# Four constants of a list scheduler's account: longer and later loads, transposes placed further back, weight-block sums one unit later

One core of one Trainium2 chip. The metric is device time in microseconds of one execution. Before: median 419.47 us of three runs (418.99 to 419.58).

## The reference

Sigmoid attention, then a gated feed-forward block:

```python
# q, k, v: [8, 12, 448, 64]; x: [3584, 768]; d_ff = 1536
scores = q @ k.transpose(0, 1, 3, 2) / 8 - log(448)
attn_out = sigmoid(scores) @ v                       # no softmax: no row sums
x = attn_out.transpose(0, 2, 1, 3).reshape(3584, 768)
g = x @ w_gate
out = (g * sigmoid(g)) * (x @ w_val) @ w_out
```

## The kernel before

The program cuts the attention into 24 units of four heads (q, k and v of one unit are 448 KB each), each with scores and the product of their sigmoids with v (PV), both in 64x64 tiles of the TensorE where all else has 128x128, and the feed-forward block into 96 pairs of a gate and a value product. The output product uses seven products for eight, for which some 128-row blocks of w_out are added and subtracted first: the **weight-block sums**, twelve instructions on DVE.

Every instruction is entered as an `Op` with an engine, a duration, its dependencies and the buffers that it takes and gives. A list scheduler plays these durations through, at each moment takes for each engine the first ready operation in a window of its queue, and emits all in the order in which it started them. The durations are an account, in the program text, of what the chip will do. On the chip every engine runs its own list in order and waits at semaphores, so a wrong duration gives no wrong result, only a poor order.

The account of loads and the constants that the change touches:

```python
class Op:
    def __init__(self, eng, dur, fn, deps=(), ..., desc=(0, 0)):
        ...
        n, size = desc                       # pieces and bytes of a piece
        self.hold = n == 1792
        self.dma = 2.0 if n == 1792 else n / 16 * max(0.042, 0.003 + size / 24600)

LAT = {"PE": 0.2, "ACT": 0.15, "DVE": 0.13, "POOL": 0.25, "SP": 1.7}
...
MARGIN = 0.0
...
# in list_schedule, for a load: the loads queue behind one another
                if o.dma:
                    dma = max(dma, now + 0.5) + o.dma
                    ...
                    o.t1 = dma + LAT["SP"]
...
# transposes on PE, units 0 to 5; -MARGIN makes them ready so much later
            a = op("PE", 0.06 * (s1 - s0), fpe(s0, s1),
                   deps=[(ins[min(k, len(ins) - 1)], -MARGIN if i > QB else 0.0)], ...)
...
    loads(0, "qk")
    ...
    loads(1, "qk")
    R["st_k", 0][1].dma += 1.0
    R["st_q", 1][0].dma += 0.4
```

The weight-block sums are drawn from a generator, one in each quarter of a unit; output products begin when the last is in the list:

```python
WSN = 1
            if i > WO + 4 or i == WO + 4 and sl > 1:      # WO = 4
                for _ in range(WSN):
                    next(wsums, None)
...
            f2acc = f2acc + 12.5 / 22.0 if f2q else 0.4
            while f2q and f2acc >= f2q[0][0] and ("ws", 4, NH - 2) in R:
                w, fn = f2q.pop(0)
                f2acc -= w
                fn(not att)
```

PE idle gaps that the account itself foresees at the start are filled with matmuls on zeros (`ps_warm`).

Of the kernel before, what the change touches and what calls it, by code (L numbers as in the profile page):

```python
# [19 lines left out]
class Slot:  # L20
# [3 lines left out]
    def __init__(self, tag):  # L24
        self.tag, self.t1 = tag, None


class Op:
# [3 lines left out]
    def __init__(self, eng, dur, fn, deps=(), mode=("F", "F"), take=(), give=(), desc=(0, 0)):  # L32
        self.eng, self.dur, self.fn, self.mode = eng, dur, fn, mode
        self.deps = [d if isinstance(d, tuple) else (d, 0.0) for d in deps if d is not None]
        self.take = [Slot(t) for t in take]
        self.give = list(give)
        self.rank = self.t0 = self.t1 = None
        n, size = desc
        self.hold = n == 1792
        self.dma = 2.0 if n == 1792 else n / 16 * max(0.042, 0.003 + size / 24600)  # L40

    def got(self, tag):
        return [s for s in self.take if s.tag == tag]
# [12 lines left out]
NEAR = 12  # L56
VIS = 9
WO = 4
MARGIN = 0.0
FREE = set()  # L60


# [90 lines left out]
def kernel(  # L153
# [70 lines left out]
    def op(*a, **kw):  # L224
        o = Op(*a, **kw)
        ops.append(o)
        return o
# [11 lines left out]
    R = {}  # L239
# [76 lines left out]
    def cast_wc(c):  # L316
        for nm in ("wg", "wv"):
            R["w16", nm, c] = [op("POOL", 0.85, fc, deps=[ld], give=ld.take)
                               for fc, ld in R["w", nm, c]]
# [8 lines left out]
    def cast_wo(f):  # L328
        R["wo16", f] = op("POOL", 0.85,
                          lambda: nc.gpsimd.tensor_copy(out=wo16[:, f], in_=T["wo", f]),  # L330
                          deps=[R["wo", f]], give=R["wo", f].take)
# [5 lines left out]
    def tr_pe(i, n, parts=None, tag="TO", split=False):  # L337

        ins = R[("cq", "ck")[n], i]
        parts = parts or [("DVE", 0, NS)]  # L340

        def fpe(s0, s1):
            def fn():
                if s0 == 0 or split:
                    T["tr", i, n] = psum.tile([128, NS, 128], BF16, tag=tag, bufs=2, name="ps_tr")
                T["tr", i, n, s0] = T["tr", i, n]
                for s in range(s0, s1):
                    nc.tensor.transpose(out=T["tr", i, n][:, s, :],  # L348
                                        in_=src16[i % NSRC][:, n, s].rearrange("p a d -> p (a d)"),
                                        identity=idn)  # L350
            return fn

        def fm(eng, s0, s1):
            def fn():
                if n == 0 and s0 == 0:
                    qkT_tile(i)
                cp(eng, T["qkT", i][:, n, s0:s1], T["tr", i, n, s0][:, s0:s1])
            return fn
        for k, (eng, s0, s1) in enumerate(parts):
            a = op("PE", 0.06 * (s1 - s0), fpe(s0, s1),  # L360
                   deps=[(ins[min(k, len(ins) - 1)], -MARGIN if i > QB else 0.0)],
                   take=[tag] if s0 == 0 or split else [], give=R["cq", i][0].take if n and s1 == NS else [])
            if s0 == 0 or split:
                bank = a.take
            m = op(eng, 0.1 + (0.53 if eng == "DVE" else 0.8) * (s1 - s0) / NS, fm(eng, s0, s1), deps=[a],
                   take=["qkT"] if n == 0 and s0 == 0 else [], give=bank if s1 == NS or split else [])
            R.setdefault(("qkT", i), []).append(m)
            R["qkT", i, n, s0] = m
# [12 lines left out]
    def burst(ds):  # L381


        def fpe():
            for i, s in ds:
                sc = psum.tile([128, 2, 512], FP32, tag="A", bufs=2, name="ps_sc")
                qT, kT = T["qkT", i][:, 0], T["qkT", i][:, 1]
                for g in range(2):
                    for a in range(2):
                        r = slice(64 * a, 64 * a + 64)  # L390
                        nc.tensor.matmul(  # L391
                            out=sc[64 * (g ^ a):64 * (g ^ a) + 64, a, 0:S].rearrange("k (s p) -> k s p", s=NS),
                            lhsT=kT[r, s, 64 * g:64 * g + 64], rhs=qT[r, :, 64 * g:64 * g + 64],
                            start=True, stop=True)
                T["sc", i, s] = sc
        give = [x for i, s in ds if s == NS - 1 for x in R["qkT", i][0].got("qkT")]
        deps = [x for i in {i for i, _ in ds} for x in R["qkT", i]]
        if ds[0][0] == 0:
            deps = [x for k, x in R.items() if k[:2] == ("qkT", 0) and len(k) > 2 and (k[2] == 0 or k[3] <= ds[0][1])]
        a = op("PE", 0.03 + 0.19 * len(ds), fpe, deps=deps,  # L400
               mode=("Q", "Q"), take=["A"] * len(ds), give=give)
        for n, d in enumerate(ds):
            sig(d, (a, 0.19 * (len(ds) - 1 - n)), a.take[n])
# [272 lines left out]
    def loads(i, which="qkv"):  # L676
        for nm in which:
            load(i, nm, {"q": q, "k": k, "v": v}[nm], [0, 3, NS] if i == 0 and nm == "k" else None)
# [7 lines left out]
    op("ACT", 1.5, lambda: nc.scalar.activation(out=warm, in_=sb_t, func=SIGM))  # L686
    loads(1, "qk")
    R["st_k", 0][1].dma += 1.0
    R["st_q", 1][0].dma += 0.4
    loads(0, "v")  # L690
    def fill(n):

# [19 lines left out]
    def bursts(i, sl):  # L712

        if i >= NQ:
            return []
        if i < QB:
            return [[(i, s)] for s in range(2 * sl, min(2 * sl + 2, NS))]
        if i < VIS and (i - QB) % 2 == 0:
            return [[(i, 2 * sl), (i, 2 * sl + 1)]] if sl < 3 else [[(i, 6), (i + 1, 0)]]
        if i < VIS:  # L720
            return [[(i, 2 * sl + 1), (i, 2 * sl + 2)]] if sl < 3 else []
        return {0: [[(i, 0), (i, 1)], [(i, 2)]], 1: [[(i, 3), (i, 4)]], 2: [[(i, 5), (i, 6)]], 3: []}[sl]
# [11 lines left out]
    for i in range(NQ + QB + 2):  # L734
        att = i < NQ
        for sl in range(4):
            if i < QB:
                nf = 0
            elif i < QB + 4:
                nf = 1 if sl < 3 else 0  # L740
            else:
                nf = min(2, max(0, 4 * (i - QB) + sl - LAG - fpos + 1))
            if i < NCW and sl == 3:
                cast_wc(i)
            if WO < i <= WO + 4 and sl == 1:
                for f in range(3 * (i - WO - 1), 3 * (i - WO)):
                    cast_wo(f)
            if i > WO + 4 or i == WO + 4 and sl > 1:
                for _ in range(WSN):
                    next(wsums, None)  # L750
            fs = []
            while len(fs) < nf and fpos < B * NF and ("xT", fpos // NF, KC - 1) in R:
                fs.append(divmod(fpos, NF))
                fpos += 1
            vals = []
            if fs and (sl or fs[0] == (0, 0)):
                vals.append(f1(*fs[0]))
            for n, ds in enumerate(bursts(i, sl)):
                if n == 1 and i >= VIS:
                    pv(i - 1)  # L760
                burst(ds)
            if sl == 0 and (i == NQ or QB < i < VIS):
                pv(i - 1)
            if sl == 0 and 0 < i < QB:
                pv(i - 1)
            if sl == 3 and i == QB - 1:
                pv(i)
            if att and i + 1 < NPE and sl in (1, 2):
                tr_pe(i + 1, sl - 1)
            if fs and not vals:  # L770
                vals.append(f1(*fs[0]))
            for n, (b, f) in enumerate(fs):
                if n:
                    vals.append(f1(b, f))
                vals[n]()
                if b % 2 == 1 and f == NF - 1:
                    f2q.extend(f2_items(b // 2))
            if att and sl == 0 and i + 2 < NQ:
                casts(i + 2)
            if att and sl == 1 and NPE <= i + 2 < NQ:  # L780
                tr_dma(i + 2)
            if sl == 1:
                if AHEAD <= i + 3 < NQ:
                    loads(i + 3)
                if WO <= i < WO + 4:
                    for f in range(3 * (i - WO), 3 * (i - WO + 1)):
                        load_wo(f)
                    uses[1] = uses[0]
# [5 lines that stand above are left out]
# [50 lines left out]
```

## Time and profile before

| | before |
|---|---|
| time, median of 3 | 419.47 us |
| time of the execution that was profiled | 420.82 us (span of the trace 419.0) |
| busy PE, DVE, ACT, POOL | 410.4, 237.7, 217.5, 133.3 us |
| DMA from 10 to 50 us | full, 375 to 382 GB/s |

Engines are PE (TensorE), DVE (VectorE), ACT (ScalarE), POOL (GpSimd), SP (SyncE, which issues the loads). The row of forty digits gives busy tenths of equal slices of the span. An instruction in order of time reads: start us, duration us, engine, line, operation, output<-input, shapes, count, and in brackets how long the engine had idled before it and whom it waited for. The lines are in the prediction below.

### The profile page before, as it was taken

To read this page: it belongs to the slowest core of one execution; us is meant where nothing else is said; L and a number is where in the kernel's file an instruction comes from. 1 tells how busy PE (TensorE), PEld (TensorE's weight loads), DVE (VectorE), ACT (ScalarE), POOL (GpSimd) and SP (SyncE) were. 2 spreads that over 40 slices of the span, in tenths; PEclk is the share of its full clock that TensorE was granted. 3 is DMA by queue.
4 is the path that set the end of the run, shared out by engine and by line. 5 is a ranking of instruction groups with operands and counts; after the bars stand their busy time and mean duration, and the time that the engine had idled before them with its cause. 6 is when DMAs were issued, how large, how long until landed. Compare 5 with 4: busy or idle time off the path is not lost.

```text
span 419.0 us, 7945 instructions
## 1 busy us (share of the span) xinstructions
PE 410.4 (98%) x3194; PEld 205.1 (49%) x3194; DVE 237.7 (57%) x420; ACT 217.5 (52%) x290; POOL 133.3 (32%) x196
## 2 busy tenths in 40 slices
PE   8989999999999999999999999999999999999995
PEld 3434444444445554544454554554545545555563
DVE  3544544467667644564574745647556465565873
ACT  5986778778751165467445565455455552122000
POOL 1788865764360232424031431403400100000000
PEclk9999999999999999999999999999999999999999
DMA  8999999997980284488067373482500302020235
GB/s 266 380 375 377 375 286 340 314 314 184 229 248 2 76 215 83 150 172 236 2 177 125 127 223 74 140 144 100 120 2 0 77 2 75 2 74 1 60 95 150
DMA packets 64693, 66.97 MB, mean 160 GB/s; under 512 B 35536, under 2 KB 60880, under 8 KB 64656
## 3 DMA queue, kind: packets, MB, share of 16 engines
q1 hardware_dynamic: 62704, 59.39, 49.7%
q0 software_dynamic: 1632, 6.69, 6.3%
q8 instruction: 25, 0.41, 0.4%
q10 hardware_dynamic: 320, 0.39, 0.3%
q14 instruction: 12, 0.10, 0.1%
HBM read 47.19 MB, written 11.01 MB: 139 GB/s over the span
## 4 chain that ended last, share of the span: by engine, by line
PE 90%; DMA 6%; DVE 1%; ACT 1%; SPq 0%; issue 0%; POOL 0%; POOLq 0%
PE ps_g L466 26%; PE ps_v L466 23%; PE ps_o L599 18%; PE ps_sc L391 8%; PE ps_pv L426 7%; PE ps_ol L599 5%; DMA st<-in_k_dram 4%; PE ps_vl L466 3%; DMA st<-in_v_dram 3%; ACT pt L408 0%; SPq L265 0%; PE ps_tr L348 0%; DVE t L476 0%; DVE hT L585 0%; POOL src L235 0%
## 5 line engine op out<-in xcount | busy, mean ns | idle before, releaser
L408 ACT ACTIVATE pt<-ps_sc,sbiast 128x896 f16<-128x896 f32 x168 | 159.0, 1007 | 28.8 <-PE ps_sc L391 28.8
L466 PE MATMUL ps_g<-xT,wg 128*128 128x448 f16 x576 | 124.0, 353 | 0.5 <-DVE t L476 0.5
L472 ACT ACTIVATE s<-ps_g 128x448 f16<-128x448 f32 x96 | 52.2, 544 | 123.5 <-PE ps_g L466 122.7
L476 DVE TENSOR_TENSOR t<-ps_g,s 128x448 f16<-128x448 f32 x96 | 59.9, 624 | 92.3 <-ACT s L472 92.2
L466 PE MATMUL ps_v<-xT,wv 128*128 128x448 f16 x504 | 109.9, 353 | 0.0
L466 PEld LDWEIGHTS <-wg 128*128 128x128 f16 x576 | 54.9, 98 | 54.8 <-issue 6.7
L466 PEld LDWEIGHTS <-wv 128*128 128x128 f16 x576 | 52.0, 98 | 59.1 <-issue 17.6
L235 POOL CAST src<-st 128x896 bf16<-128x896 f32 (+1 forms) x43 | 40.3, 937 | 96.8 <-DMA st<-in_q_dram 66.7
L482 DVE SCALAR_TENSOR_TENSOR hT<-ps_v,t 128x448 f16<-128x448 f32 x84 | 52.4, 624 | 32.0 <-PE ps_v L466 31.1
L391 PE MATMUL ps_sc<-qkT 64*64 64x448 bf16 x672 | 50.8, 360 | 0.8 <-ACT pt L408 0.6
L599 PEld LDWEIGHTS <-hT 128*128 128x128 f16 x384 | 37.6, 98 | 27.2
L235 POOL CAST v<-st 64x448 f16<-64x448 f32 (+1 forms) x72 | 42.2, 586 | 22.4 <-DMA st<-in_v_dram 8.7
L614 POOL DMA_DIRECT2D out_dram<-osb x34 | 17.7, 525 | 93.6 <-DVE osb L604 93.5
L426 PE MATMUL ps_pv<-pt,v 64*64 64x448 f16 x672 | 37.7, 351 | 0.2
L604 DVE SCALAR_TENSOR_TENSOR osb<-ps_o,osb 128x384 f32<-128x384 f32 x63 | 34.0, 551 | 6.2 <-PE ps_o L599 6.2
L233 DVE CAST xT<-ps_pv 128x448 f16<-128x448 f32 x40 | 23.4, 619 | 20.7 <-PE ps_pv L426 20.7
L599 PE MATMUL ps_o<-wo,hT 128*128 128x384 f16 x168 | 31.9, 326 | 0.0
L391 PEld LDWEIGHTS <-qkT 64*64 64x64 bf16 x672 | 14.8, 105 | 29.0 <-issue 25.2
L426 PEld LDWEIGHTS <-v 64*64 64x64 f16 x672 | 19.3, 107 | 14.6 <-issue 3.8
L599 PE MATMUL ps_o<-st,s 128*128 128x384 f16 x138 | 26.2, 326 | 0.0
L599 PE MATMUL ps_o<-st,hT 128*128 128x384 f16 x138 | 26.2, 326 | 0.0
L599 PEld LDWEIGHTS <-s 128*128 128x128 f16 x168 | 16.4, 98 | 11.8
(44 smaller groups left out, 195.6 us busy)
## 6 DMA issues: line engine op xcount, KB each, us to landing
st<-in_q_dram SPq DMA_DIRECT2D x24, 448.0 KB, 5.3
st<-in_v_dram SPq DMA_DIRECT2D x24, 448.0 KB, 6.3
st<-in_k_dram SPq DMA_DIRECT2D x23, 448.0 KB, 5.5
out_dram<-osb POOLq DMA_DIRECT2D x34, 192.0 KB, 3.1
st<-in_moe_w_gate_dram SPq DMA_DIRECT2D x12, 384.0 KB, 8.8
st<-in_moe_w_val_dram SPq DMA_DIRECT2D x12, 384.0 KB, 8.8
st<-in_moe_w_out_dram SPq DMA_DIRECT2D x12, 384.0 KB, 6.9
out_dram<-st SPq DMA_DIRECT2D x16, 192.0 KB, 2.7
```

The source lines that it names most:

```text
L233: nc.vector.tensor_copy(out=o, in_=i)
L235: nc.gpsimd.tensor_copy(out=o, in_=i)
L391: nc.tensor.matmul(out=sc[64 * (g ^ a):64 * (g ^ a) + 64, a, 0:S].rearrange("k (s p) -> k s p", s=NS), lhsT=kT[r, s, 64 * g:64 * g + 64], ...
L408: nc.scalar.activation(out=pt, in_=T[("sc",) + key][:, :, 0:S], func=SIGM, bias=sb_t, scale=qkscale)
L426: nc.tensor.matmul(out=T["pv", i, a][64 * g:64 * g + 64, :], lhsT=T["v16", i][r, a, s, :], rhs=T["pt", i, s][r, a, :], start=(s == 0), sto ...
L466: nc.tensor.matmul(out=T[nm, b, f], lhsT=w[c][:, j, ff * 128:(ff + 1) * 128], rhs=T["xT", b, j], start=(j == 0), stop=(j == KC - 1))
L472: nc.scalar.activation(out=t, in_=T["g", b, f], func=SIGM)
L476: nc.vector.tensor_tensor(out=t, in0=T["g", b, f], in1=T["s16", b, f], op=MULT)
L482: nc.vector.scalar_tensor_tensor(out=T["hT", m][:, f, o * S:(o + 1) * S], in0=T["v", b, f], scalar=HSC, in1=T["t1", b, f], op0=MULT, op1=MULT)
L599: nc.tensor.matmul(out=T["p", m, k, n], lhsT=lhs()[:, x // 2, x % 2], rhs=rhs(x), start=x == 0, stop=x == NH - 1)
L604: C[name] = op("DVE", 0.45, lambda: nc.vector.scalar_tensor_tensor(out=c(*dst), in0=T["p", m, k, n], scalar=HREC, in1=c(*other), op0=MULT, ...
L614: dma.dma_start(out=out[rows, cols].rearrange("(p s) d -> s p d", s=NS)[s], in_=T[("osb",) + t][64 * x:64 * x + 64, cols])
```

## The change

The intent is an account closer to the chip: loads that take longer and land later at the start, transposes that are not queued before their cast is done, weight-block sums that do not stand in DVE's way so early. The whole diff:

```diff
--- before.py
+++ after.py
@@ -37,7 +37,7 @@
         self.rank = self.t0 = self.t1 = None
         n, size = desc
         self.hold = n == 1792
-        self.dma = 2.0 if n == 1792 else n / 16 * max(0.042, 0.003 + size / 24600)
+        self.dma = 2.0 if n == 1792 else n / 16 * max(0.042, size / 22300 - 0.003)
 
     def got(self, tag):
         return [s for s in self.take if s.tag == tag]
@@ -56,7 +56,7 @@
 NEAR = 12
 VIS = 9
 WO = 4
-MARGIN = 0.0
+MARGIN = 1.0
 FREE = set()
 
 
@@ -686,7 +686,7 @@
     op("ACT", 1.5, lambda: nc.scalar.activation(out=warm, in_=sb_t, func=SIGM))
     loads(1, "qk")
     R["st_k", 0][1].dma += 1.0
-    R["st_q", 1][0].dma += 0.4
+    R["st_q", 1][0].dma += 1.0
     loads(0, "v")
     def fill(n):
 
@@ -745,7 +745,7 @@
             if WO < i <= WO + 4 and sl == 1:
                 for f in range(3 * (i - WO - 1), 3 * (i - WO)):
                     cast_wo(f)
-            if i > WO + 4 or i == WO + 4 and sl > 1:
+            if i > WO + 5 or i == WO + 5 and sl > 1:
                 for _ in range(WSN):
                     next(wsums, None)
             fs = []
```

## The prediction

> **What bounds the kernel now.** I read the page's busy times first, then the 40 slices, then the waits of the TensorE, and last the instructions in order of time.
>
> The page before, totals and slices:
>
> ```profile
> PE 410.4 (98%) x3194; PEld 205.1 (49%) x3194; DVE 237.7 (57%) x420; ACT 217.5 (52%) x290; POOL 133.3 (32%) x196
> ...
> PE   8989999999999999999999999999999999999995
> ...
> ACT  5986778778751165467445565455455552122000
> ...
> DMA  8999999997980284488067373482500302020235
> ```
>
> PE is busy 98%, every other engine under 60%. PE's row falls below 9 only in slices 0 and 2 and in the last, the stores' tail. So nothing can be won from slice 3 on by making anything else faster, only by running PE's work with fewer gaps before about 31 us. That start is also where DMA is full (9 of 10 from slice 1 to 8).
>
> Busy is not useful, though. The group of filler matmuls keeps PE busy at the start and computes nothing:
>
> ```profile
> L696 PE MATMUL ps_warm<-wide 128*128 128x512 bf16 x26 | 9.2, 450 | 1.2 <-DVE wide L195 1.2
> ```
>
> They lie between 1.2 and 18.7 us. Filler costs nothing where PE had nothing to do, but it shows how much of the start PE only waits. The stages (stretch, then busy time of PE, PEld, DVE, ACT, POOL, then clock, DMA share, GB/s) tell who holds the start:
>
> ```profile
> 10.00:20.00 10.00, 9.77 (x126) 4.60 (x127) 5.67 (x9) 8.90 (x11) 6.64 (x11) 1.00 1.06 382
> 20.00:30.00 10.00, 8.50 (x104) 3.92 (x97) 3.56 (x6) 9.49 (x12) 8.41 (x12) 1.00 1.06 375
> 30.00:40.00 10.00, 9.74 (x75) 4.16 (x76) 4.97 (x9) 6.52 (x10) 8.43 (x12) 1.00 1.07 376
> 40.00:50.00 10.00, 10.00 (x108) 4.96 (x104) 5.35 (x9) 7.08 (x10) 8.48 (x12) 1.00 1.06 376
> ```
>
> From 10 to 30 us ACT (the sigmoids of the first three units, 21 of about 1.0 us) and DMA (375 to 382 GB/s) are both near full; PE misses 1.50 us in 20:30 and 0.26 us in 30:40, and has none to give after. All PE waits with a named releaser between 15 and 35 us are these:
>
> ```profile
> PE ps_tr L348 <- POOL src L235: 0.9, 2, 0.7
> PE ps_sc L391 <- ACT pt L408: 0.6, 2, 0.4
> PE ps_tr L348 <- DVE xT L233: 0.2, 1, 0.2
> ```
>
> The first is unit 4's transposes, of q at 29.50 us and of k at 30.70 us, each standing in PE's queue before its cast has finished. In order of time:
>
> ```profile
> 29.50 0.56 PE L348 MATMUL ps_tr<-idn,src 128*128 128x128 bf16 x7 [0.68 <-POOL src L235]
> ...
> 30.70 0.56 PE L348 MATMUL ps_tr<-idn,src 128*128 128x128 bf16 x7 [0.26 <-POOL src L235]
> ```
>
> After 35 us the only named PE waits are 0.3 us at 66.2 and 0.24 us at 120.0, both on a DVE product.
>
> **What the Trainium skill says.** "TensorE: Matmul & The Clock Gate", Part 1, architectural detail: matmuls stay in program order, only weight loads are pulled ahead, and ACT and DVE queues are strict FIFO. The trace agrees: scores issued at 10.08 us sit behind transposes at 9.58 that waited for a cast, while ACT idled 0.50 us. So order is all this change alters. "TensorEngine Tiling (Array Packing)", Key Properties: changing the tiling mode drains the engine. The trace agrees: eight score matmuls advance the chain by 0.38 us right after a PV group (same 64x64 mode), by 0.50 us after a 128x128 group, and the next group of six then takes 1.24 instead of 1.14: 0.12 + 0.10 = 0.22 us for one excursion. "DMA: Bandwidth & Descriptors", Specifications, gives about 358 GB/s of HBM per core and 435 for the fabric; this trace has 375 to 382. "Perfetto Trace Analysis", Identifying the Most-Contended Engine, warns that matmul busy time is a bad measure; the filler above is this trace's example.
>
> **The change part by part.** No instruction, byte or buffer of the computation is added or removed. The program holds a list scheduler with an account of durations; its account sets each engine's order, and the number of filler matmuls. I use the account's constants only to see which decisions flip.
>
> (a) Loads longer and later. A q, k or v load of 1792 B pieces goes from 16 x (0.003 + 1792/24600) = 1.214 to 16 x (1792/22300 - 0.003) = 1.238 us; a weight load from 1.047 to 1.054; q of unit 1 gets 0.6 more. One round of three unit loads and six weight loads grows from 9.92 to 10.04. On the chip the q loads are issued at 19.71, 29.63 and 39.55 us, a round of 9.92: the old length was right, the old offset was not. Summing, q of unit 1 lands at 8.16 in the old account, 8.78 in the new; its cast starts at 8.90 on the chip. k of unit 1: 9.38, 10.02, chip 10.09. k of unit 4: 27.8, 28.7, chip 29.7. So the new account is nearer everywhere in the start. Flips I expect: scores before transposes around 9.5 us, and perhaps around 16.5. ACT's idle gaps there are 0.50 us (before 10.52) and 0.60 us (before 17.50), 1.10 together, in a stage where ACT is the bound. I credit half, 0.5 us, because the loads bound the same stage.
>
> (b) Transposes 1.0 us later after their cast, for units above 3 that still use PE: units 4 and 5, four groups of seven. Unit 5's (42.8 and 46.1 us) wait for nothing already. Unit 4's waited 0.68 + 0.26 = 0.94 us. At 28.8 us two value matmuls (0.38 us of array time; they ran at 29.90) and soon the next gate group (1.14) were available to go first. I credit 0.7 us of 0.94.
>
> (c) The twelve weight-block sums (DVE, 0.63 to 0.68 us each, about 7.9 us) start at 92.64 and end at 115.3 us. One unit is about 10.2 us there (PV at 93.53, 103.80, 113.95), so they move to about 103 to 125, and the first output product from 121.1 to about 130. DVE is 8.30 of 10 busy in 90:100 yet PE is 10.00 of 10 in that stretch: moving them frees nothing on PE. The one wait near it (0.24 us at 119.99) can vanish or recur. PE without output products keeps full as it did from 75 to 115. Credit 0.0.
>
> (d) Price. With PE about 1 us earlier after 31 us, data can be late: the last value-weight cast of the second quarter ends at 37.96 and its first matmuls start at 38.59, a slack of 0.63 us. Charge 0.1 us, as some other work can go first.
>
> Sum: -0.5 - 0.7 + 0.0 + 0.1 = -1.1 us. 419.47 - 1.1 = 418.4.
>
> **The rivals.** *The loads take the gain back.* DMA is full to 50 us; if everything PE does before 50 us is paced by landings, the removed 0.94 us reappears as waits on casts of weights or of unit 5. For it: the 0.63 us slack and three weight-load waits of 0.4 us each (hidden under busy PE). Against it: PE was 10.00 of 10 in 40:50, so it runs behind the loads, not on them. Then 419.2 to 419.5. *A worse order.* The new load length is 0.12 us per round too long, so over four rounds 0.5 us of work may be put off needlessly, the sums may collide with the first halves of the output products on DVE, and a few more mode excursions at 0.22 us each may arise. Then 419.7 to 420.5. *More than I see.* If both ACT gaps close wholly, unit 4's waits go and some late excursions merge, 1.1 + 0.94 + 0.5 = 2.5 us: 417.0. *A large change* by over 2% is 8.4 us. Gains cannot reach that: all PE idle is 419.0 - 410.4 = 8.6 us, of which about 4 is the stores' tail and 1.2 the program's start. A loss of 8.4 us would need PE starved in the middle, with DVE, ACT and DMA all below 60% there; I see no cause.
>
> **Range and chances.** Centre 418.4; the first rival and run spread (418.99 to 419.58) give 419.9 above, the third gives 417.1 below. Faster by over 2%: 0.01; within: 0.98; slower: 0.01.
>
> **What would show it.** (a) right: ACT's idle before its runs near 10.5 and 17.5 us shrinks below 0.2 us, and PV of unit 3 (39.83 us before) comes about 1 us earlier. (b) right: no PE wait of transposes on POOL near 30 us; PE busy in 20:30 above 9.0. (c) right: sums start near 102, first output product near 130, PE still 10.00 of 10 in 90 to 140. (d): a new PE wait on a weight cast between 35 and 50 us would be the charge. The prediction is wrong if PE shows waits between 60 and 400 us that were not there, if the number of switches between score and full-array groups changes by more than five, or if PV of unit 3 comes later than before.

## The result

| | before | changed |
|---|---|---|
| median, first comparison (6 runs each) | 419.49 us | 419.26 us |
| lowest and highest | 418.99, 420.74 | 419.13, 419.99 |
| median, second comparison (11 and 6 runs) | 419.62 us | 419.72 us |

A ratio is the mean time of one kernel's fast runs over that of the other's fast runs of the same rounds, so it is not quite the ratio of these medians. It is 0.9995 (95% interval 0.998 to 1.0011) in the first comparison and 1.0003 (0.9988 to 1.0018) in the second: the same time. The predicted ratio, 418.4 / 419.47 = 0.9974, lies below both intervals; 419.26 and 419.72 lie inside the predicted range.

The page of the changed kernel, totals and slices, to be read against those of before:

```profile
PE 409.9 (98%) x3192; PEld 205.4 (49%) x3194; DVE 237.5 (57%) x420; ACT 217.5 (52%) x290; POOL 132.7 (32%) x196
...
PE   8989999999999999999999999999999999999995
...
ACT  6977777878775103577445465455455552122000
...
DMA  8999999997977026387067383472500302020235
```

The shape is the same. PE counts two matmuls fewer, but its weight loads (PEld) are 3194 in both, and the second profile of the changed kernel has all 26 fillers: two records are missing from this trace, and the programs have equally many. The stages of the changed kernel (stretch, then busy PE, PEld, DVE, ACT, POOL, clock, DMA share, GB/s):

```profile
20.00:30.00 10.00, 8.74 (x99) 4.14 (x95) 4.28 (x7) 8.38 (x11) 7.96 (x11) 1.00 1.06 375
30.00:40.00 10.00, 10.00 (x102) 4.76 (x102) 4.81 (x8) 7.02 (x9) 8.33 (x12) 1.00 1.07 376
```

Against the first profile of before, PE gained 0.24 us in the first stretch and 0.26 in the second. The PE waits with a named releaser between 15 and 35 us in the changed kernel (us in total, times, longest):

```profile
PE ps_sc L391 <- ACT pt L408: 0.7, 2, 0.4
PE ps_g L466 <- DVE t L476: 0.5, 1, 0.5
PE ps_tr L348 <- DVE xT L233: 0.2, 1, 0.2
```

The wait of transposes on POOL is gone. In its place a gate product waits for DVE. In order of time:

```profile
29.14 1.29 PE L466 MATMUL ps_g<-xT,wg 128*128 128x448 f16 x6 [0.45 <-DVE t L476]
...
30.87 0.56 PE L348 MATMUL ps_tr<-idn,src 128*128 128x128 bf16 x7
```

And ACT, whose chain of 21 sigmoids had gaps of 0.50 and 0.60 us in the first profile of before, now has none that the view lists (one of 0.11 us is below its limit):

```profile
6.24 19.26 ACT L408 ACTIVATE pt<-ps_sc,sbiast 128x896 f16<-128x896 f32 x21 [0.48 <-PE ps_sc L391]
```

Read against the first profile of before alone, this is a success: the PV group of unit 3 starts at 38.64 us instead of 39.83, the last matmul group at 412.18 instead of 413.66, and the span falls from 419.0 to 417.5, all of 1.2 to 1.5 us. The unprofiled runs do not show it. One of the two must mislead. The load queue says which. Issues by SP in the first profile of before:

```profile
7.13 0.98 SPq L265 DMA_DIRECT2D st<-in_q_dram  x1
8.89 0.37 SPq L265 DMA_DIRECT2D st<-in_k_dram  x1
```

and in the changed kernel:

```profile
6.67 0.50 SPq L265 DMA_DIRECT2D st<-in_q_dram  x1
7.53 0.37 SPq L265 DMA_DIRECT2D st<-in_k_dram  x1
```

The k load of unit 3 waits for the q load of unit 1 to land (issued at 8.89 us, landed at 8.88; in the changed kernel 7.53 and 7.51), and so it is a clock of the landings. It came 1.36 us earlier, although the changed kernel's own list of loads is the same up to there.

### The profile page after: what moved, and what is told of

Same layout as the page of the kernel before. It is cut to its first block, busy times and chain, and to the rows that moved or that the text cites. A ratio compares the mean times of both kernels' runs of the same rounds, so it can differ in the third digit from the quotient of the medians.

```text
span 417.5 us, 7938 instructions
## 1 busy us (share of the span) xinstructions
PE 409.9 (98%) x3192; PEld 205.4 (49%) x3194; DVE 237.5 (57%) x420; ACT 217.5 (52%) x290; POOL 132.7 (32%) x196
## 4 chain that ended last, share of the span: by engine, by line
PE 93%; ACT 5%; DVE 1%; issue 0%; ACTq 0%
PE ps_g L466 26%; PE ps_v L466 24%; PE ps_o L599 18%; PE ps_sc L391 9%; PE ps_pv L426 7%; PE ps_ol L599 5%; ACT pt L408 4%; PE ps_vl L466 3%; PE ps_warm L696 1%; PE ps_tr L348 1%; DVE t L476 0%; ACT s L472 0%; DVE st L604 0%; ACT qkT L231 0%; ACT xT L231 0%
```

## The experiments

Twelve kernels. Kernels are compared only within the same rounds.

**A measure that scatters less.** All profiles showed one pattern, which I use below. Let *start* be the beginning of the fourth gate product and *middle* the time from the thirteenth to the forty-first. From the fourth to the thirteenth it took 32.23 us in every kernel (32.22 in one). Time minus start minus middle is 277.9 to 278.0 us in every profile without an extra load. So the time is start + middle + a constant, and whatever a part does shows in one of two terms. By the fourth gate product both kernels have done the same matmuls (108 score, 84 PV, 70 transposes, 18 gate, 18 value), so starts compare fairly. (The last expectations give the constant as 277.7: there the start was counted from another zero.)

| profile | k load of unit 3 issued | start | middle | time |
|---|---|---|---|---|
| before, first | 8.89 | 36.86 | 105.98 | 420.82 |
| before, again | 7.80 | 35.22 | 106.15 | 419.28 |
| loads part | 8.74 | 36.18 | 107.69 | 421.83 |
| transposes part | 8.16 | 35.87 | 106.52 | 420.38 |
| sums part | 7.64 | 35.33 | 105.69 | 418.95 |
| loads + transposes | 8.85 | 36.71 | 106.13 | 420.77 |
| changed, first | 7.53 | 35.67 | 105.69 | 419.31 |
| changed, again | 7.80 | 36.03 | 105.69 | 419.67 |
| before, extra load | 8.27 | 35.65 | 106.10 | 419.91 |
| changed, extra load | 7.87 | 36.11 | 105.69 | 420.05 |
| offset + sums, first | 8.01 | 37.74 | 105.69 | 421.39 |
| offset + sums, again | 7.50 | 34.88 | 105.69 | 418.55 |
| changed, POOL copies | 7.90 | 36.13 | 105.69 | 419.78 |
| changed, POOL memsets | 8.05 | 35.83 | 105.70 | 419.45 |

Each line is one execution. With the later sums the middle is 105.69 to 105.70 in all eight; without them it scatters, from 105.98 to 107.69. The last six lines belong to parts 4 to 6.

### 1. The kernel before, again

No edit.

> The kernel before, unchanged, measured against itself, with a fresh profile. Theory L (late landing): the first profile of before was taken in an execution of 420.82 us, 1.3 us over its median, in which the loads of unit 1 landed about 1.2 us later than in the profile of after; nothing in the kernel caused it. Then the fresh profile has its cast of q of unit 1 near 7.9 us (8.90 in the first), a span near 417.7 us (419.0), and waits of unit 4's transposes on their casts below 0.3 us (0.94). Theory O (order): the late landing comes from before's own order; then the fresh profile repeats 8.9 us, 419.0 us and 0.94 us. Both: ratio 1.000, the interval giving the noise, about 0.001 each way.

Measured: 419.86 us (419.28 to 420.48), ratio 1.0007 (0.9995 to 1.0019). The fresh profile's load queue:

```profile
7.80 0.37 SPq L265 DMA_DIRECT2D st<-in_k_dram  x1
```

its ACT:

```profile
6.48 10.20 ACT L408 ACTIVATE pt<-ps_sc,sbiast 128x896 f16<-128x896 f32 x11 [0.56 <-PE ps_sc L391]
16.87 9.26 ACT L408 ACTIVATE pt<-ps_sc,sbiast 128x896 f16<-128x896 f32 x10 [0.20 <-PE ps_sc L391]
```

and its PE at the transposes of unit 4's k:

```profile
29.06 0.56 PE L348 MATMUL ps_tr<-idn,src 128*128 128x128 bf16 x7
```

The same program, with the k load 1.09 us earlier, has no wait before these transposes (0.26 us in the first profile; the 0.68 us before q's transposes are gone as well), ACT gaps of 0.20 us instead of 1.10 among those listed, and a span of 417.5. PE is busy 9.07 us in 20:30, more than the 8.74 of the changed kernel. So the waits that I had credited belonged to one execution. Theory L (late landing) stands, theory O (the order causes the landing) falls. The cast of q of unit 1 started at 8.19 us, not the 7.9 that I expected; the direction is the same. What makes the loads land late is not shown: the first bytes of the loads move at 1.8 us in all profiles, and between 10 and 12 us the rate is alike (378 to 405 GB/s). The difference arises between: from 4 to 5 us the rate is 199 to 311 GB/s.

### 2. The parts alone

The loads part alone:

```diff
-        self.dma = ... n / 16 * max(0.042, 0.003 + size / 24600)
+        self.dma = ... n / 16 * max(0.042, size / 22300 - 0.003)
-    R["st_q", 1][0].dma += 0.4
+    R["st_q", 1][0].dma += 1.0
```

> Only the load part: load length 0.003 + size/24600 becomes size/22300 - 0.003, and 0.6 more for q of unit 1. Theory L: 419.2 to 419.5, ratio within 0.0007 of 1, as ACT's two gaps are mostly absent in a usual execution. Rival T (taken back: parts gain at the start and the sums give it back): 418.8 to 419.1, that is 0.4 to 0.6 us faster.

Measured: 420.33 us (419.35 to 422.36), ratio 1.0026 (1.0006 to 1.0046): slower, which neither theory expected. PE, DVE and POOL in order of time in the stretch where it is lost:

```profile
92.51 2.69 POOL L330 CAST wo<-st 128x768 f16<-128x768 f32 x3
...
93.67 1.94 DVE L523 TENSOR_TENSOR st<-wo 128x768 f16<-128x768 f16 x2
...
97.54 1.75 DVE L523 TENSOR_TENSOR st<-wo,st 128x768 f16<-128x768 f16 x2
97.60 2.48 POOL L235 CAST src<-st 128x896 bf16<-128x896 f32 x2 [2.39 <-DMA st<-in_q_dram]
99.21 0.61 DVE L476 TENSOR_TENSOR t<-ps_g,s 128x448 f16<-128x448 f32 x1
...
99.87 1.30 PE L466 MATMUL ps_g<-xT,wg 128*128 128x448 f16 x6 [1.22 <-DVE t L476]
```

Two pairs of weight-block sums take 1.94 and 1.75 us beside casts on POOL, where a sum elsewhere takes 0.55. The gate's DVE product at 99.21 stands behind the second pair, and PE waits 1.22 us for the PSUM bank that this product frees. A second such wait, 0.53 us, comes at 121.0. That is the middle of 107.69. It is one execution, and not every one can have it: the fastest run, 419.35 us, would then have started at 33.7, and no profile shows a start before 34.88.

The transposes part alone:

```diff
-MARGIN = 0.0
+MARGIN = 1.0
```

> Only the transposes part: MARGIN 0 becomes 1. Theory L: 419.2 to 419.5, at most 0.3 us faster, because the wait before unit 4's transposes is short in a usual execution. Rival T: 418.7 to 418.9, the 0.7 us that the prediction credited.

Measured: 420.44 us (418.89 to 420.99), ratio 1.0017 (1.0001 to 1.0033). No gain here either: middle 106.52, with waits on the DVE product of 0.26 us at 98.6 and 0.48 at 119.6. Both theories expected a gain or nothing. Rival T is refuted for this part, and theory L missed the loss in the middle.

The sums part alone:

```diff
-            if i > WO + 4 or i == WO + 4 and sl > 1:
+            if i > WO + 5 or i == WO + 5 and sl > 1:
```

> Only the sums part: the weight-block sums enter the order one unit later. Theory L: 419.3 to 419.6, no effect (0.24 us at most, the one wait on a DVE product near 120 us). Rival T: 420.3 to 420.6, about 1 us slower, the part that gives back what the two others gain.

Measured: 419.43 us (418.95 to 419.57), ratio 0.9994 (0.9982 to 1.0005). By time this cannot be told from nothing, and certainly not from the 1 us slower of rival T. By the middle it can: 105.69, against 105.98 and 106.15. All named PE waits after 36 us, first in the first profile of before, then with the sums part:

```profile
PE ps_g L466 <- DVE t L476: 0.5, 2, 0.3
PE ps_g L466 <- DVE t L476: 0.3, 1, 0.3
```

The one that is gone is the 0.24 us at 119.99; the one that is left, near 65 us, lies before the thirteenth gate product in every profile.

### 3. The first two parts together

The diff of the change without the sums part.

> The change without its sums part: loads and transposes together. Theory R (repair): these two parts rearrange the start without gain in a usual execution and bring the weight-block sums beside casts on POOL, so DVE's gate product is late and PE waits; the sums part is there to repair that. Then this is slower than before by 0.4 to 1.0 us (ratio 1.001 to 1.0025), with 0.5 us or more of PE waits on the DVE product between 90 and 125 us. Rival N (noise): each single part's slowness was scatter of the start; then the ratio is within 0.0007 of 1 and such waits stay below 0.4 us.

Measured: 420.74 us (419.49 to 420.98), ratio 1.0018 (1.0005 to 1.0032). Slower by the amount of theory R, but not for its reason: the one such wait is 0.24 us and the middle is 106.13, no worse than before's. The loss is in the start. So the reading that the sums part repairs damage of these two falls for the pair: the loads part alone (107.69) and the transposes part alone (106.52) lost in the middle of the one execution that was profiled, both together did not, and there the sums part removes 0.44 us (106.13 to 105.69), about what it removes from before. Each single part with the sums part was not run. The start also shows how far it scatters: this program has the changed kernel's order on every engine up to the first weight-block sum, long after the fourth gate product, and yet its median gives a start of 36.7 us, where the changed kernel's two give 35.6 and 36.1 (how, is worked out in part 4).

### 4. Late landings on purpose

Before and changed kernel, each with one more load, not used, ahead of unit 1's q:

```diff
+                if i == 1 and nm == "q":
+                    nc.sync.dma_start(
+                        out=spare.rearrange("p (h d) -> p h d", h=4),
+                        in_=src[0][0:4, 0:128, :].rearrange("h p d -> p h d"))
```

> The kernel before with one more load of 128 KB in 512 pieces of 256 B put ahead of unit 1's q load; its data is not used, no other engine's order changes. It makes the landings of unit 1 late by some 1 us on purpose. Theory L: time rises by about the delay, 0.8 to 1.4 us, and the profile shows again what the first profile of before showed: transposes of unit 4 waiting 0.5 to 1 us on POOL and ACT idle 0.5 us or more near 10.5 and 17.5 us. Rival (the first profile's waits belonged to that chip or moment): time rises under 0.4 us, as PE has filler in the start to give.

> The changed kernel with the same extra load. Theory P (the prediction's mechanism holds where landings are late): its order was made for landings 0.6 us later, so it rises by 0.3 to 0.8 us less than the kernel before with the same extra load, and is faster than that one by 0.5 to 1.0 us. Rival F (fully paced by landings): it rises as much, 0.8 to 1.4 us, and the two late kernels are within 0.3 us of each other.

Measured: before with the load 420.49 us (ratio to before 1.0015, 1.0001 to 1.0028), changed with the load 419.99 (1.0001, 0.9987 to 1.0014). In the profile of the first, the k load of unit 3 came at 8.27 us, only 0.47 later than in the fresh profile of before, so the delay was smaller than meant, and so were its marks: one wait of unit 4's transposes of 0.21 us, ACT gaps of 0.2. The 0.5 us between the two late kernels is what theory P wants at its lower end, but the intervals overlap. Inconclusive.

The table of profiles says more. In executions with the k load issued at 7.80 us, before starts at 35.22 and the changed kernel at 36.03, 0.81 later. With early loads otherwise, the order of before (sums part, 7.64) has 35.33 and the changed kernel (7.53) 35.67. With late loads, before (8.89) has 36.86, and the changed kernel's start order (loads + transposes, 8.85) 36.71, earlier by 0.15. From early to late, before's start moves by 36.86 - 35.22 = 1.64 us for 1.09 us of lateness, the changed order's by 36.71 - 36.03 = 0.68 for 1.05. These are single executions. They fit one reading, that the new start order is made for late landings and loses where they are early; they do not show it. The clock is not complete either: with the k load at 8.01 and 8.05 us, two kernels started at 37.74 and 35.83, the first because loads of unit 0 were late. Over many runs the start follows as median time minus middle minus 277.95, with 106.1 for before's middle: first comparison 35.4 and 35.6, second 35.6 and 36.1. By this the changed kernel starts 0.2 and 0.5 us later. But the kernel before, measured against itself, came out 0.28 us above itself (419.86 and 419.58), and the sums part, whose list of matmuls is before's until long after the fourth gate product, gives 35.8 beside 35.5. So 0.2 us cannot be told from scatter, and 0.5 only just. What speaks for a price is that all four early profiles of the changed start order without an extra load (35.67 to 36.13) lie above both early ones of before's order (35.22 and, with the sums part, 35.33).

Where such a price would come from is not shown. One candidate are the switches between the 64x64 and the 128x128 mode before the fourth gate product, fillers left out: 20 in every profile of before and 24 in every one of the changed kernel, because scores and PV are cut apart by transposes and single products. At 0.22 us for two, four would be 0.44 us. Against it: the version in part 5 has 24 as well, and one of its profiles has the earliest start of all, 34.88. The other candidate is the gate product's wait of 0.45 us at 29.14, which all six profiles of the changed start order show (0.45 or 0.46) and that version does not.

### 5. The changed kernel again, and a version that might beat both

> The changed kernel again, on the chip of the next three runs. In all profiles so far the time is start + middle + 277.7 us, where start is when the fourth gate product begins and middle the way from the thirteenth to the forty-first gate product: before has middle 105.98 and 106.15, the changed kernel 105.69. Theory S (two small terms): middle again 105.69, 0.3 to 0.5 us under before; start the same as before's on average; so 0.2 to 0.5 us faster than before, ratio 0.9988 to 0.9996. Rival N: middle scatters and the ratio is 1.000 within 0.0004.

Measured: 419.72 us (419.4 to 420.54), ratio 1.0003 (0.9988 to 1.0018). The middle is 105.69 again, as theory S says; the start is not the same as before's but later, so the gain of 0.2 to 0.5 us did not come. Half right.

The version takes the offset of unit 1's q, the old load length, no margin, later sums. Against before:

```diff
-    R["st_q", 1][0].dma += 0.4
+    R["st_q", 1][0].dma += 1.0
-            if i > WO + 4 or i == WO + 4 and sl > 1:
+            if i > WO + 5 or i == WO + 5 and sl > 1:
```

> A version that might beat both: only 0.6 us more for q of unit 1 (the offset that the landings bear out), the old load length (a round of loads was 9.92 us both in the account and on the chip), no margin for transposes, sums one unit later. Theory R: no switch is added by the margin and the sums do not collide; 418.8 to 419.3, 0.2 to 0.5 us faster than before. Rival N: 419.3 to 419.7, the same.

> The version with the offset of q of unit 1 and the later sums only, again, since its first run had one execution of 421.39 among five of 418.65 to 419.55. It lacks the two places where the margin puts transposes behind a gate product that waits 0.45 us. Theory S: middle 105.69, start 0.2 to 0.4 us earlier than the changed kernel's on average: 418.8 to 419.2. Rival N: the same as the changed kernel within 0.2 us.

Measured: 419.04 us beside 419.82 for before (ratio 0.9991, 0.9972 to 1.0011), and 419.29 beside 419.62 (0.9993, 0.9976 to 1.001). The middle is 105.69 in both and there is no wait of 0.45 us; the switches are 24 as well, so these alone do not make a start late. Both times it is some 0.3 to 0.8 us ahead by the medians, and both intervals hold 1. The expected 0.2 to 0.5 us are neither shown nor refuted. One of its executions, of 421.39 us, had the loads of unit 0 late (transposes of k of unit 0 waited 0.77 us). A better version is not shown.

### 6. Why sums beside POOL are slow

The changed kernel with two POOL instructions more at each weight-block sum, once copies from SBUF, once memsets; the orders of PE, DVE, ACT and SP are unchanged:

```diff
                 R["ws", j, c] = op("DVE", 0.56, ...)
+                for _ in range(2):
+                    op("POOL", 0.02, lambda: nc.gpsimd.tensor_copy(out=spare, in_=wo16[:, 0, 0:512]),
+                       deps=[(R["ws", j, c], 5.0)])      # or: nc.gpsimd.memset(spare, 0.0)
```

> The changed kernel with 24 copies of 128x512 16-bit from SBUF to a scratch on POOL, two at each weight-block sum; their result is not used, and no order but POOL's changes. Theory K (the sums lose time to POOL's reads of SBUF, which is what moving them saves): sums beside these copies take 0.8 to 1.1 us instead of 0.55, their mean rises over 0.8, and middle grows by 0.3 us or more. Rival D (DVE is only crowded, by number of instructions): sums stay at their durations and middle at 105.7.

> The same with 24 memsets of the scratch in place of the copies: POOL writes SBUF but reads nothing. Theory K: the sums are not stretched by them, mean as in the changed kernel (0.67 to 0.75), middle within 0.1 of 105.7. Rival W (any work on POOL stretches them): as with the copies.

With the copies, DVE and POOL in order of time:

```profile
93.93 3.49 POOL L531 COPY spare<-wo 128x512 f16<-128x512 f16 x4
94.48 0.79 DVE L524 TENSOR_TENSOR st<-wo,st 128x768 f16<-128x768 f16 x1
95.73 0.54 DVE L524 TENSOR_TENSOR st<-wo 128x768 f16<-128x768 f16 x1
...
121.17 2.17 POOL L531 COPY spare<-wo 128x512 f16<-128x512 f16 x3
121.19 1.00 DVE L524 TENSOR_TENSOR st<-wo 128x768 f16<-128x768 f16 x1
```

and the copies as a group (count, then shortest, median and longest in ns, first and last start in us):

```profile
L531 POOL COPY spare<-wo x24: 608/613/938, 93.9 to 128.4; 128x512 f16<-128x512 f16 x24
```

With the memsets, in order of time and as a group:

```profile
120.15 2.27 POOL L531 MEMSET spare<- 128x512 f16 x4
120.89 0.55 DVE L524 TENSOR_TENSOR st<-wo 128x768 f16<-128x768 f16 x1
```

```profile
L531 POOL MEMSET spare<- x24: 518/524/525, 93.7 to 127.1; 128x512 f16 x24
```

Beside a copy a sum takes up to 1.00 us, or it keeps 0.54 and the copies stretch instead, up to 938 ns from 613, or both stretch a little (0.79 us at 94.48). Beside memsets alone neither stretches: sums at 0.55 to 0.56, all 24 memsets at 518 to 525 ns. This is what the Trainium skill says in "SBUF — State Buffer", Who interferes with whom: a DVE instruction with two SBUF inputs contends with a GpSimd instruction that reads SBUF, not with one that only writes, and whichever issues first makes the other wait.

But the times are 419.73 and 420.02 us (ratios to before 1.0000 and 1.0004), the mean sum rose to 0.71 us only (0.65 in the changed kernel, 0.66 with memsets), not over 0.8, and **the middle stayed, at 105.69 and 105.70**. So theory K is right on instructions and wrong on the time: where the sums are spread, some stretched ones cost nothing. The sums part shows the same: its sums took 0.75 us in the mean, longer than before's 0.64 to 0.65, and its middle was 105.69. In the fresh profile of before, seven sums lie in the 6.2 us from 91.00 on; in the changed kernel three lie in the first 2.2 us from 93.16 and the next begins at 100.43. That the crowd at one place, with casts beside it, is what PE ends up waiting for is what the loads part shows (1.22 us). How much of it is the number of sums and how much their stretch was not separated.

## Why the prediction was right or wrong

The class, within 2%, and the range, 417.1 to 419.9, held; that is luck more than insight, for the upper end of the range was the first rival and the run spread. The gain of 1.1 us did not come, and two of the prediction's own signs of being wrong appeared: the switches changed by six, over the five allowed, and PV of unit 3 came later than in the fresh profile of before.

- **What bounds the kernel**: PE, right. That time can be won "only by running PE's work with fewer gaps before about 31 us" was wrong: the one sure gain lies between 90 and 125 us. From the fourth gate product to the thirteenth, and from the forty-first to the end, no part of the change moved anything by 0.1 us.
- **Step (b), "Unit 4's waited 0.68 + 0.26 = 0.94 us ... I credit 0.7 us"**: this step failed, by its size. The wait measured 0.94 us in a late execution and under the reporting limit in the fresh profile of the same kernel (0.26 us in all with the sums part). The mechanism worked, the wait is gone in the changed kernel, but a wait of 0.45 us on DVE stands in its place, so PE's busy time in 20:30 is 8.74 and not above 9.0 as I had set as a sign.
- **Step (a), -0.5 us**: the flips came as foreseen, scores before transposes, and ACT runs 21 sigmoids without a listed gap. But the listed gaps were 0.20 us in the fresh profile, not 1.10, so half of 1.10 was too much. That PV of unit 3 came 1.2 us earlier was my sign for this step, and it deceived: in the fresh profile of before it starts at 38.19, earlier than the changed kernel's 38.64.
- **Step (c), "moving them frees nothing on PE ... Credit 0.0"**: wrong. It freed 0.29 to 0.46 us in the middle, the one gain that repeats in every profile. The "0.63 to 0.68 us each" are means: in the first profile of before nine of the twelve took 0.54 to 0.64 us and three 0.88 to 1.00. The sums began at 93.16 and not at about 103, because they were spread rather than moved; the end, 125.3, and the first output product, at 132.06 (I said about 130), were near. I saw PE at 10.00 of 10 in 90:100 and stopped; one wait was at 119.99, which I had listed and set down as neutral, and a further one was too short to be listed (a gate product at 99.29 that stands 1.26 us after the value product before it instead of 1.14).
- **Step (d), +0.1 us**: no wait on a weight cast appeared.
- **The rival of a worse order** named mode excursions at 0.22 us. They came, 150 switches became 156, four of them in the start, but what they cost here is not shown (part 4). The 0.22 us itself is borne out, though not every term: eight scores after a PV group and before a 128x128 group advance by 0.48 us, not 0.38 (0.38 is twice the 0.19 of four scores between PV groups), and the group that takes 1.23 to 1.24 is the one before a 64x64 group, not the one after.
- **A section of the skill**: that matmuls stay in program order, which the prediction cites from Part 1 of "TensorE: Matmul & The Clock Gate", is stated in Part 2, Step-by-step.

The sum as it turned out: the middle gives 0.3 to 0.5 us, the credited waits were mostly absent from a usual execution, and the time stays. That the start takes the 0.3 to 0.5 us back is likely, not shown.

## What to carry to other kernels

Compare the time of the profiled execution with the median before crediting any of its waits; if it is slower by as much as the gain in question, profile the kernel again. When the time scatters more than the effect, look for marks in the trace between which nothing scatters: here two intervals carried all of the difference, and in the kernels with later sums one repeated to 0.01 us where the total varied by over 1. An order fitted to the landings of one execution may fit that execution alone.

## What the Trainium skill lacked or had wrong

- No page tells how much landings vary between executions of one kernel ("DMA: Bandwidth & Descriptors" would be the place): the same k load was issued at 7.80 and at 8.89 us, with like rates of 375 to 382 GB/s afterwards (10 to 50 us), and the start moved by 1.64 us. That rate is also above the 358 GB/s of HBM per core that its Specifications give (one core ran here); the measurement decides.
- "TensorEngine Tiling (Array Packing)", Key Properties, says that a mode switch drains the engine but gives no cost: 0.12 us into and 0.10 us out of the 64x64 mode here, by the starts of the matmuls.
- "SBUF — State Buffer", Who interferes with whom, agrees with the runs here; what it lacks is the size of the stretch for 16-bit sums: from 0.55 us alone up to 1.00 beside a copy of 0.61 us, and the copy up to 0.94.
